# Attention and two expert layers on one core: the loop over experts put outside the loop over token groups

## The chip, the core and the metric

The kernel runs on one core of one Trainium2 chip. The metric is the time of one execution on the device in microseconds (us); of several runs the median is taken. The engines are TensorE (PE in the rows; PEld is its weight load), VectorE (DVE), ScalarE (ACT), GpSimd (POOL) and SyncE (SP), which here only issues transfers.

## The reference

Three stages follow one another: attention with a memory, a dense layer of two matrix products, and four experts of the same form whose results are mixed.

```python
# 1: q, k, v (2, 8, 576, 64); local is causal softmax attention
attn = g * mem_out + (1 - g) * local            # -> x (1152, 512)
# 2: dense layer, w_in (512, 2048), w_out (2048, 512)
r = np.maximum(x @ w_in, 0.0)
x = (r * r) @ w_out
# 3: E = 4 experts, w1 (4, 512, 1024), w2 (4, 1024, 512)
p = domain_probs / (domain_probs.sum(-1, keepdims=True) + 1e-09)
for e in range(E):
    h = np.maximum(x @ w1[e], 0.0)
    out += p[:, e:e + 1] * (h @ w2[e])
```

## The kernel before, in words

The 1152 tokens are nine tiles of 128. Attention and the dense layer run in three chunks of tiles; the experts run in two token groups, c = 0 with tiles 0 to 3 (512 tokens) and c = 1 with tiles 4 to 8 (640 tokens). The change is in the experts and in the last chunk of the dense layer, `ffn1(2, ...)`, which runs beside the first preparations for the experts.

**Blocks and pairs.** An expert's 1024 hidden units are cut into four blocks p of 256. `w2[e * 4 + p, half]` holds a block's weights as raw float32, 512 KB for the first matrix (half 0, "up") and 512 KB for the second (half 1, "down"). `pairs` lists (c, e, p): 32 pairs, the token group outermost, so that each block is met twice.

**A block's preparation.** `fetch(i, half)` (L873) issues the load of a raw block on SP. `square(i, half)` (L825) sums its squares on ACT, for an expert's scale. `w_power(e)` (L817) adds these sums up over partitions with a PE product by ones and makes powers of two of them on DVE (`power`); `prep_up` and `prep_down` scale by them. `prep_down` (L902) splits the down weights into a high and a low half in float16: two ACT copies (L832) and two DVE instructions (L833). `prep_up` (L879) does it for seven combinations of the up weights, since a product of 2 x 2 sub-blocks is done in seven sub-products: four sums on POOL into `ws` (L891 to L896, one buffer), two ACT copies into `wu` (L893, L899) and three DVE low parts (L888). The token side has the same splits: `tokens(c)` (L839) makes seven split operands `xs` out of four subtractions `tt` (L850), seven ACT copies and seven DVE instructions (L832, L833).

**A pair's products.** `up2(i)` (L912) issues seven products of six matmuls (L924) into PSUM banks taken in turn from `spots`; ACT copies two of them (p1 at L947, p5 at L953, which frees their banks), DVE adds the others up (L945), POOL adds one term (u4 at L954). `hidden(m)` (L936) then makes the hidden values: ACT's Relu gives the high half (L939), DVE the low half (L940). `down2(i)` (L1000) multiplies the hidden values by the down weights, three matmuls of 512 columns for each tile and half m (L1016), into one PSUM bank per tile (`o0` to `o4`); after an expert's last block `drain` (L1024) scales the bank and adds it to `acc` on DVE (L1029), and after the last expert issues the output transfer (L1035).

**Order.** PE executes in the order of the program. The other engines' instructions are put in order by a scheduler, which goes by priority in program order and by when it expects an instruction to be ready; an instruction under `tc.keep_in_program_order` keeps its place. Each engine executes its instructions strictly in the order that results, so that one that waits holds up all behind it. The loop at the end of the program makes one step for each pair i: the steps of `up2(i)` are spread among those of `down2(i - 1)`, and after each one a step of the next preparation is issued, with squares at fixed places:

```python
        fetch(i + 6, 0)
        fetch(i + 6, 1)
...
        ahead = chain(prep_down(i), prep_up(i + 1))
        for n, g in enumerate(steps):
            next(g)
            next(ahead, None)
            if n in (5, 7, 9, 11):
                square(*next(todo, (len(pairs), 0)))
```

Raw blocks have 6 and 7 buffers, `wu` has 2, the split down weights 2. In the last dense chunk the loop over `ffn1(2, ...)` issues the fetches of blocks 0 to 5 and the squares of blocks 0 to 3, the scale of expert 0, the splits of the first token group, the preparation of the first up weights, and in its last steps the products of the first pair (`up_0`). That chunk's own weights are rounded on ACT (L83) and their low half is made on POOL or DVE (L84); its Relu, square and split are L706, L707, L712 and L713, its matmuls L106 and L723.

## Time and profile before

| | us |
|---|---|
| median of 3 runs | 743.21 (741.28 to 744.14) |
| the profiled execution, its own time | 740.5 |
| its span, first to last instruction | 738.7 |
| PE busy | 686.9 (93%) |
| DVE busy | 549.1 (74%) |
| ACT busy | 430.2 (58%) |
| POOL busy | 241.4 (33%) |

The profile's times count from the first instruction of the span. A busy share is an average over stages: attention and the dense layer run until about 375 us, the first token group of the experts until about 525 us, the second to the end. In a row of the timeline the number in brackets is the idle time of the engine just before, with what ended it.

### The profile page before, as it was taken

How to read it: one execution, taken by the hardware profiler on the slowest of the kernel's cores; microseconds unless marked ns; L12 is line 12 of the kernel's file. 1: busy time of each engine (PE TensorE's matmuls, PEld its weight loads, DVE VectorE, ACT ScalarE, POOL GpSimd, SP SyncE). 2: the span in 40 equal slices, each digit the busy share in tenths (PEclk: the TensorE clock that was granted, in tenths of full speed). 3: DMA queues.
4: the chain of work that ended last, by engine and by line, in shares of the span. 5: the costliest groups of instructions: out<-in, count | busy, mean ns of one | idle time of the engine just before them, and what ended most of it. 6: DMA issues, size and time to landing. Idle time of an engine off the chain costs nothing.

```text
span 738.7 us, 12576 instructions
## 1 busy us (share of the span) xinstructions
PE 686.9 (93%) x4604; PEld 487.1 (66%) x4604; DVE 549.1 (74%) x1057; ACT 430.2 (58%) x844; POOL 241.4 (33%) x249
## 2 busy tenths in 40 slices
PE   6588899989899998999999989999999999999997
PEld 4466777767677787989865655566655555555553
DVE  4867858479989874746879968989787685867763
ACT  5687767376665534887776756655535353535341
POOL 1101101253533237645623433344432323141400
PEclk7799999999999999999999999999999999999999
DMA  9788765177885543685412323233342222100002
GB/s 286 229 297 289 254 219 180 58 262 222 196 197 122 122 114 83 238 302 169 131 59 93 108 85 115 87 113 94 109 168 75 100 81 91 58 1 1 1 1 71
DMA packets 65422, 101.25 MB, mean 137 GB/s; under 512 B 32656, under 2 KB 34704, under 8 KB 65360
## 3 DMA queue, kind: packets, MB, share of 16 engines
q1 hardware_dynamic: 65216, 100.45, 44.5%
q8 instruction: 36, 0.59, 0.3%
q14 instruction: 26, 0.21, 0.1%
q10 hardware_dynamic: 144, 0.00, 0.0%
HBM read 82.87 MB, written 10.75 MB: 127 GB/s over the span
## 4 chain that ended last, share of the span: by engine, by line
PE 52%; DVE 18%; ACT 11%; DMA 9%; issue 6%; POOL 3%; SPq 0%; DVEq 0%; ACTq 0%; POOLq 0%
PE o L1016 19%; PE pe L924 16%; DMA raw<-in_w 4%; PE y L723 3%; PE hpb L106 3%; PE pv L584 2%; DMA wraw<-w1s 2%; DVE bits L661 2%; PE y L721 2%; POOL w L84 2%; PE hpa L101 2%; DVE g L713 1%; ACT a L320 1%; DVE a L189 1%; PE sc L516 1%
## 5 line engine op out<-in xcount | busy, mean ns | idle before, releaser
L1016 PE MATMUL o<-w,g 128*128 128x512 f16 x864 | 218.5, 379 | 7.0 <-DVE g L940 3.8
L924 PE MATMUL pe<-xs,wu 128*128 128x256 f16 (+1 forms) x1344 | 196.5, 286 | 2.1 <-DVE h L945 2.0
L924 PEld LDWEIGHTS <-wu 128*128 128x128 f16 x1344 | 131.0, 98 | 70.3 <-issue 3.8
L1016 PEld LDWEIGHTS <-g 128*128 128x128 f16 x864 | 83.7, 98 | 77.8 <-DVE g L940 7.1
L84 POOL TENSOR_TENSOR w<-wraw,w 128x512 fp32r<-128x512 f32 x49 | 73.1, 1498 | 104.6 <-ACT w L83 104.3
L939 ACT ACTIVATE g<-h 128x512 f16<-128x512 f32 (+1 forms) x64 | 43.3, 677 | 105.7 <-DVE h L945 105.7
L723 PE MATMUL y<-g,w 128*128 128x512 f32 (+1 forms) x384 | 90.7, 372 | 1.5 <-ACT w L83 0.7
L954 POOL TENSOR_TENSOR u<-u,p 128x256 f32<-128x256 f32 (+1 forms) x32 | 32.3, 1011 | 132.7 <-ACT p L953 110.9
L723 PEld LDWEIGHTS y<-g,w 128*128 128x128 f32 x384 | 68.2, 189 | 9.7 <-ACT w L83 1.0
L940 DVE SCALAR_TENSOR_TENSOR g<-h,g 128x512 f16<-128x512 f32 (+1 forms) x64 | 50.4, 788 | 26.3 <-ACT g L939 26.0
L106 PE MATMUL hpb<-x,w 128*128 128x512 f32 x192 | 53.2, 414 | 4.7 <-DVE r L707 4.6
L945 DVE SCALAR_TENSOR_TENSOR h<-pe,u 128x256 f32<-128x256 f32 (+1 forms) x96 | 42.8, 451 | 19.8 <-PE pe L924 15.7
L891 POOL TENSOR_TENSOR ws<-raw 128x256 f32<-128x256 f32 x32 | 23.3, 727 | 101.9 <-issue 88.7
L888 DVE SCALAR_TENSOR_TENSOR wu<-ws,wpow,wu 128x512 f16<-128x512 f32 x64 | 50.9, 835 | 2.9 <-ACT wu L899 2.9
L833 DVE SCALAR_TENSOR_TENSOR w<-raw,wpow,w 128x512 f16<-128x512 f32 x64 | 48.0, 755 | 0.7 <-ACT w L832 0.6
L83 ACT ACTIVATE w<-wraw 128x512 fp32r<-128x512 f32 x64 | 39.5, 623 | 13.0 <-DMA wraw<-w1s 6.6
L106 PEld LDWEIGHTS hpb<-x,w 128*128 128x128 f32 x192 | 36.3, 196 | 13.6 <-DVE r L707 6.4
L832 ACT ACTIVATE w<-raw,wpow 128x512 f16<-128x512 f32 x64 | 44.6, 709 | 0.9 <-PE o L1016 0.9
L829 ACT ACTIVATE junk<-raw 128x1024 bf16<-128x1024 f32 x32 | 33.5, 1048 | 19.0 <-DMA raw<-in_w 18.9
L189 DVE CUSTOM_DVE_ANT_0 a<-sc,mask 128x384 f32<-128x384 f32 (+4 forms) x80 | 35.9, 477 | 11.1 <-PE sc L303 5.5
L204 POOL TENSOR_TENSOR xm<-xm,cf 128x512 f32<-128x512 f32 x9 | 10.6, 1184 | 102.1 <-ACT at L337 42.7
L106 PE MATMUL hpc<-x,w 128*128 128x384 f32 x192 | 37.3, 339 | 3.1 <-POOL w L84 2.0
(159 smaller groups left out, 1200.0 us busy)
## 6 DMA issues: line engine op xcount, KB each, us to landing
raw<-in_w SPq DMA_DIRECT2D x64, 512.0 KB, 3.4
w<-in_w SPq DMA_DIRECT2D x32, 512.0 KB, 4.4
wraw<-w1s SPq DMA_DIRECT2D x64, 256.0 KB, 3.1
w1s<-bits SPq DMA_DIRECT2D x32, 256.0 KB, 2.5
kraw<-in_kc SPq DMA_DIRECT2D x8, 576.0 KB, 4.1
vraw<-in_vc SPq DMA_DIRECT2D x8, 320.0 KB, 3.7
qraw<-in_qc SPq DMA_DIRECT2D x4, 512.0 KB, 4.9
out<-acc SPq DMA_DIRECT2D x8, 256.0 KB, 2.1
```

What stands on the lines that cost most here:

```text
L84: eng.tensor_sub(w[:, 1], raw, w[:, 0].bitcast(F32))
L106: nc.tensor.matmul(acc, lhsT=w[:, a, kk * P:(kk + 1) * P], rhs=xs_r[c][:, b, kk, :], start=(i == 0), stop=(i == 3 * NK - 1),)
L189: nc.vector.tensor_tensor_reduce(out=dst, in0=sc, in1=msk, op0=ALU.add, op1=ALU.max, scale=1.0, scalar=-3.0e38, accum_out=m)
L723: nc.tensor.matmul(yacc[d], lhsT=w[:, a, d * P:(d + 1) * P], rhs=g[:, b], start=(first and i == 0), stop=(last and i == 2),)
L832: nc.scalar.activation(out=w0, in_=x, func=AF.Copy, scale=s)
L833: nc.vector.scalar_tensor_tensor(out=w1, in0=x, scalar=s, in1=w0, op0=ALU.mult, op1=ALU.subtract)
L888: nc.vector.scalar_tensor_tensor(out=w[:, 1, ks], in0=x, scalar=s1, in1=w[:, 0, ks], op0=ALU.mult, op1=ALU.subtract)
L924: nc.tensor.matmul(acc, lhsT=w[:, wa, k, kk * P:kk * P + P], rhs=x[:, xb, kk], start=(m == 0), stop=(m == 5))
L939: nc.scalar.activation(out=g[:, 0], in_=hm, func=AF.Relu)
L940: nc.vector.scalar_tensor_tensor(out=g[:, 1], in0=hm, scalar=0.0, in1=g[:, 0], op0=ALU.max, op1=ALU.subtract)
L945: nc.vector.scalar_tensor_tensor(out=out, in0=acc, scalar=HID, in1=x, op0=ALU.mult, op1=ALU.add)
L1016: nc.tensor.matmul(outs[t], lhsT=g[:, gb, r:r + P], rhs=w[:, wa], start=(p == 0 and m == 1 and k == 0), stop=(p == 3 and m == 0 and k == 2),)
```

## The change

The loops over experts and token groups change places: `pairs` runs over e, then c, then p, so that a block is prepared once, into one of five `wu` buffers and one of five buffers for down weights, and used by both groups. `blocks` lists (e, p), and `fetch`, `square`, `prep_up` and `prep_down` go by block q. Raw blocks have four buffers each; a block's preparation itself issues the fetch of the block four later. The blocks of the next expert are squared in steps 1 to 4 of an expert's eight, pinned in program order, one at place 9 of a step and one at its end; its scale is made in step 5 and its blocks are prepared in steps 5, 6, 7 and 0. The splits of the second token group come in steps 2 and 3 of the whole loop. The fourth product bank (`o4`) is taken back for three steps of each first group. For an expert's last block `down2` goes tile by tile, and the sums of the second group get a place of their own (`late_acc`).

```diff
-    pairs = [(c, e, p) for c in range(2) for e in range(ne) for p in range(4)]
+    blocks = [(e, p) for e in range(ne) for p in range(4)]
+    pairs = [(c, e, p) for e in range(ne) for c in range(2) for p in range(4)]
...
-    def square(i, half):
-        if i < len(pairs):
-            c, e, p = pairs[i]
-            if c == 0:
-                nc.scalar.activation(out=junk2, in_=raws[i, half], func=AF.Square, accum_out=wsq[:, e, half, p:p + 1])
+    def square(q, half):
+        e, p = blocks[q]
+        tc.keep_in_program_order(
+            nc.scalar.activation(out=junk2, in_=raws[q, half], func=AF.Square, accum_out=wsq[:, e, half, p:p + 1])
+        )
...
-    def fetch(i, half):
-        if i < len(pairs):
-            _, e, p = pairs[i]
-            raw = raws[i, half] = xp.tile([P, 2 * DM], F32, tag=f"raw{half}", name=f"raw{half}", bufs=6 + half)
-            nc.sync.dma_start(out=raw, in_=w2[e * 4 + p, half])
+    def fetch(q, half):
+        if q < len(blocks):
+            raw = raws[q, half] = xp.tile([P, 2 * DM], F32, tag=f"raw{half}", name=f"raw{half}", bufs=4)
+            nc.sync.dma_start(out=raw, in_=w2[q, half])
...
-        w = wus[i] = xp.tile([P, 2, 7, 2 * P], F16, tag="wu", name="wu")
+        w = wus[q] = xp.tile([P, 2, 7, 2 * P], F16, tag="wu", name="wu", bufs=5)
...
+        fetch(q + 4, 0)
         low(w, s[:, 2:4], slice(5, 7))
...
-        w = wp.tile([P, 2, DM], F32R, tag="w0", name="w0").bitcast(F16)
+        if q % 5 == 4:
+            w = acp.tile([P, 2, DM], F32R, name="w2").bitcast(F16)
+        else:
+            w = wp.tile([P, 2, DM], F32R, tag=f"w{q % 5 % 2}", name="wd").bitcast(F16)
...
+        fetch(q + 4, 1)
+
+    def prep(q):
+        yield from prep_down(q)
+        yield from prep_up(q)
...
-            if 8 <= i < 56 and i % 4 == 0:
+            if 8 <= i < 40 and i % 4 == 0:
                 fetch((i - 8) // 8, i // 4 % 2)
...
+        if p == 3:
+            todo.sort(key=lambda x: 2 * x[0] - 3 * x[1])
...
+    late_acc = xyp.tile([P, NT - LAST, DM], F32, tag="x2", name="acc")
+    n_e = 2 * 4
...
-        fetch(i + 6, 0)
-        fetch(i + 6, 1)
-        todo = iter([(j, half) for j in {0: (), 1: (4, 5), 2: (6, 7)}.get(i, (i + 5,)) for half in range(2)])
...
-        ahead = chain(prep_down(i), prep_up(i + 1))
+        spots[3:] = [(ps_o, "o4")] if c == 0 and (p or not i) else []
...
+        step, ahead, todo = i % n_e, iter(()), []
+        if e == 0 and c == 0:
+            ahead = chain(prep_down(p), *([prep_up(p + 1)] if p < 3 else []))
+        elif i >= n_e - 3:
+            q = 4 * ((i - n_e + 3) // n_e + 1) + (i - n_e + 3) % n_e
+            if (i - n_e + 3) % n_e < 4 and q < len(blocks):
+                ahead = prep(q)
+        if 1 <= step <= 4 and e + 1 < ne:
+            todo = [(4 * (e + 1) + step - 1, half) for half in range(2)]
         for n, g in enumerate(steps):
             next(g)
-            next(ahead, None)
-            if n in (5, 7, 9, 11):
-                square(*next(todo, (len(pairs), 0)))
+            if step != 5 or n > 3:
+                next(ahead, None)
+            if n == 9 and todo:
+                square(*todo.pop(0))
...
-            if n == 14 and i < 4 * ne - 4 and i % 4 == 2:
-                w_power(pairs[i + 2][1], bank([P, 8], "wt").rearrange("p (m n) -> p m n", m=2))
-        if i >= 5 and steps:
-            next(side, None)
+            if (i == 2 and n % 3 == 2) or (i == 3 and n % 3 < 2):
+                next(side, None)
+            if n == 2 and step == 5 and e + 1 < ne:
+                w_power(e + 1, bank([P, 8], "wt").rearrange("p (m n) -> p m n", m=2))
         run(ahead)
+        if todo:
+            square(*todo.pop(0))
```

Three places of the order that results are shown, before and after; the line numbers are each program's own.

ACT before, in the loop's sixth step (L829 is a square, L939 the Relu of the hidden values, L947 and L953 the copies p1 and p5, L832 and L893 and L899 copies of weights):

```order
L829 ACTIVATE junk2_3277,wsq_3276<-raw0_4793 128x1024
L939 ACTIVATE g1_4766<-h1_4668 128x512
L829 ACTIVATE junk2_3277,wsq_3276<-raw1_4795 128x1024
L832 ACTIVATE w0_4812<-raw1_4137,wpow_3274 128x512
L939 ACTIVATE g0_4780<-h0_4667 128x512
L947 ACTIVATE p1_4799<-pe_4804 128x256
```

ACT after, in steps 4 and 5 of the second expert (L946 is the Relu, L954 p1, L960 p5, L833, L891 and L897 the copies of weights):

```order
L829 ACTIVATE junk2_3277,wsq_3276<-raw0_5078 128x1024
L946 ACTIVATE g1_5521<-h1_5444 128x640
L946 ACTIVATE g0_5536<-h0_5443 128x640
L829 ACTIVATE junk2_3277,wsq_3276<-raw1_5051 128x1024
L954 ACTIVATE p1_5546<-pe_5551 128x320
L833 ACTIVATE wd_5599<-raw1_4711,wpow_3274 128x512 x2
L891 ACTIVATE wu_5618<-raw0_4738,wpow_3274 128x768
L960 ACTIVATE p5_5547<-pe_5607 128x320
L897 ACTIVATE wu_5618<-ws_5619,wpow_3274 128x1024
L891 ACTIVATE wu_5716<-raw0_4835,wpow_3274 128x768
```

One square now stands ahead of the two Relus and one behind them; three copies that need the new expert's scale stand ahead of p5, and the copies of two blocks stand in one step.

POOL before, at the end of the dense layer (L891 to L896 are sums of up weights, block 1's and block 2's; L84 is the low half of the last dense block but one; L954 is u4 of the first pair):

```order
L896 TENSOR_TENSOR ws_4145<-raw0_3405,ws_4145 128x256
L84 TENSOR_TENSOR w1_3973<-wraw_3927,w1_3973 128x512
L891 TENSOR_TENSOR ws_4197<-raw0_3457 128x256
L895 TENSOR_TENSOR ws_4197<-raw0_3457 128x256
L892 TENSOR_TENSOR ws_4197<-ws_4197,raw0_3457 128x256
L896 TENSOR_TENSOR ws_4197<-raw0_3457,ws_4197 128x256
L954 TENSOR_TENSOR u4_4016<-u2_4014,p5_4013 128x256
```

POOL after, the same place (L889 to L894 are the sums, L961 is u4):

```order
L894 TENSOR_TENSOR ws_4138<-raw0_3405,ws_4138 128x256
L889 TENSOR_TENSOR ws_4190<-raw0_3457 128x256
L893 TENSOR_TENSOR ws_4190<-raw0_3457 128x256
L890 TENSOR_TENSOR ws_4190<-ws_4190,raw0_3457 128x256
L894 TENSOR_TENSOR ws_4190<-raw0_3457,ws_4190 128x256
L84 TENSOR_TENSOR w1_3965<-wraw_3919,w1_3965 128x512
L889 TENSOR_TENSOR ws_4318<-raw0_3506 128x256
L893 TENSOR_TENSOR ws_4318<-raw0_3506 128x256
L890 TENSOR_TENSOR ws_4318<-ws_4318,raw0_3506 128x256
L894 TENSOR_TENSOR ws_4318<-raw0_3506,ws_4318 128x256
L961 TENSOR_TENSOR u4_4010<-u2_4008,p5_4007 128x256
```

Block 2's four sums moved ahead of the dense layer's low half, and block 3's four ahead of the first pair's u4.

ACT after, the end of the dense layer up to p1 of the first pair (L83 is the dense layer's rounding, L706 and L712 its Relu and split; `ws_4138` and `ws_4190` are blocks 1 and 2, `raw0_3506` is block 3):

```order
L897 ACTIVATE wu_4137<-ws_4138,wpow_3274 128x1024
L891 ACTIVATE wu_4317<-raw0_3506,wpow_3274 128x768
L706 ACTIVATE r_3944<-hpc_3926 128x384
L833 ACTIVATE wd_4130<-raw1_3385,wpow_3274 128x512 x2
L712 ACTIVATE g_3947<-r_3944 128x384
L83 ACTIVATE w1_3965<-wraw_3919 128x512
L897 ACTIVATE wu_4189<-ws_4190,wpow_3274 128x1024
L706 ACTIVATE r_3983<-hpc_3968 128x384
L833 ACTIVATE wd_4299<-raw1_3482,wpow_3274 128x512 x2
L712 ACTIVATE g_3986<-r_3983 128x384
L83 ACTIVATE w1_4019<-wraw_3924 128x512
L954 ACTIVATE p1_4006<-pe_4011 128x256
```

Before, the copies of blocks 2 and 3 stood behind the first pair's first Relu; here both blocks have one ahead of p1 (`wu_4317`, `wu_4189`).

## Rows read from the trace of the kernel before

**Rows 1.** Busy time by stretch: stretch, length, then PE, PEld, DVE, ACT, POOL, clock, DMA.

```profile
377.00:525.00 148.00, 140.61 (x938) 91.01 (x937) 126.46 (x248) 91.97 (x159) 58.77 (x70) 1.00 0.30 97
525.00:724.00 199.00, 198.71 (x1182) 115.34 (x1180) 142.85 (x236) 85.22 (x130) 57.79 (x77) 1.00 0.18 59
```

**Rows 2.** Timeline of PE, dense layer: start, length, engine, line, shapes [idle before].

```profile
326.40 0.61 PE L106 MATMUL hpc<-x,w 128*128 128x384 f32 x2 [0.41 <-ACT w L83]
...
333.59 2.02 PE L106 MATMUL hpc<-x,w 128*128 128x384 f32 x10 [0.84 <-POOL w L84]
```

**Rows 3.** Timeline of ACT, dense layer and sixth step of the experts.

```profile
321.55 1.04 ACT L829 ACTIVATE junk<-raw 128x1024 bf16<-128x1024 f32 x1
...
325.73 1.14 ACT L83 ACTIVATE w<-wraw 128x512 fp32r<-128x512 f32 x2
...
428.12 1.06 ACT L829 ACTIVATE junk<-raw 128x1024 bf16<-128x1024 f32 x1 [5.33 <-DMA raw<-in_w]
```

**Rows 4.** Timeline of PE, experts' loop.

```profile
396.92 0.81 PE L924 MATMUL pe<-xs,wu 128*128 128x256 f16 x6 [0.26 <-DVE h L945]
...
409.26 0.61 PE L1016 MATMUL o<-w,g 128*128 128x512 f16 x2 [0.33 <-DVE g L940]
...
429.84 0.39 PE L1016 MATMUL o<-w,g 128*128 128x512 f16 x1 [0.96 <-ACT g L939]
...
533.33 1.79 PE L924 MATMUL pe<-xs,wu 128*128 128x320 f16 x12 [0.29 <-DVE h L945]
```

**Rows 5.** Groups by shape, 377 to 733 us: busy us, mean ns | idle before.

```profile
L888 DVE SCALAR_TENSOR_TENSOR wu<-ws,wpow,wu 128x512 f16<-128x512 f32 x60 | 47.0, 824 | 0.3 <-ACT wu L899 0.3
L833 DVE SCALAR_TENSOR_TENSOR w<-raw,wpow,w 128x512 f16<-128x512 f32 x60 | 44.5, 744 | 0.7 <-ACT w L832 0.6
L832 ACT ACTIVATE w<-raw,wpow 128x512 f16<-128x512 f32 x60 | 41.9, 709 | 0.9 <-PE o L1016 0.9
L899 ACT ACTIVATE wu<-ws,wpow 128x1024 f16<-128x1024 f32 x30 | 34.1, 1137 | 0.0
L888 DVE SCALAR_TENSOR_TENSOR wu<-raw,wpow,wu 128x768 f16<-128x768 f32 x29 | 29.7, 1023 | 6.1 <-ACT wu L893 5.6
L893 ACT ACTIVATE wu<-raw,wpow 128x768 f16<-128x768 f32 x29 | 27.0, 930 | 14.3 <-PE pe L924 11.1 <-DVE wpow L134 3.3
...
L940 DVE SCALAR_TENSOR_TENSOR g<-h,g 128x512 f16<-128x512 f32 x31 | 23.0, 741 | 14.2 <-ACT g L939 14.1
...
L945 DVE SCALAR_TENSOR_TENSOR h<-pe,u 128x256 f32<-128x256 f32 x45 | 18.2, 414 | 4.4 <-PE pe L924 3.1 <-POOL u L954 1.2
...
L829 ACT ACTIVATE junk<-raw 128x1024 bf16<-128x1024 f32 x16 | 16.8, 1051 | 18.4 <-DMA raw<-in_w 18.4
...
L833 DVE SCALAR_TENSOR_TENSOR xs<-tt,ypow,xs 128x640 f16<-128x640 f32 x4 | 4.4, 1088 | 0.0
...
L850 DVE TENSOR_TENSOR tt<-y 128x640 f32<-128x640 f32 x2 | 1.6, 818 | 0.0
```

**Rows 6.** Timeline of all engines, dense layer to experts.

```profile
360.56 1.15 ACT L899 ACTIVATE wu<-ws,wpow 128x1024 f16<-128x1024 f32 x1 [2.73 <-POOL ws L896]
...
364.30 0.95 PE L723 MATMUL y<-g,w 128*128 128x384 f32 x2 [0.74 <-ACT w L83]
...
364.32 1.56 POOL L84 TENSOR_TENSOR w<-wraw,w 128x512 fp32r<-128x512 f32 x1 [3.79 <-ACT w L83]
364.67 1.76 DVE L888 SCALAR_TENSOR_TENSOR wu<-ws,wpow,wu 128x512 f16<-128x512 f32 x1
...
366.51 0.73 POOL L891 TENSOR_TENSOR ws<-raw 128x256 f32<-128x256 f32 x1 [0.63 <-DVE wu L888]
...
371.46 0.81 PE L924 MATMUL pe<-xs,wu 128*128 128x256 f16 x6 [1.30 <-DVE h L945]
```

**Rows 7.** Timeline of all engines, end.

```profile
731.18 3.39 DVE L1029 SCALAR_TENSOR_TENSOR acc<-o,prs,acc 128x512 f32<-128x512 f32 x5 [2.41 <-PE o L1016]
731.96 3.62 SPq L1035 DMA_DIRECT2D out<-acc  x6
```

More of the change, by code (lines that the diff above doesn't have):

```diff
@@ L986, in attention_then_experts @@
                 next(up_0, None)
+        run(side)
         run(up_0)
@@ L1011, in down2 @@
         todo = [(t, m) for m in (1, 0) for t in range(t0, t1)]
+        if p == 3:
+            todo.sort(key=lambda x: 2 * x[0] - 3 * x[1])
         for t, m in todo:
-            g, w = gs[i, m], wds[i, m]
+            g, w = gs[i, m], wds[4 * e + p, m]
             r = (t - t0) * P
@@ L1025, in drain @@
         if e == 0:
-            acc[t] = acp.tile([P, DM], F32, tag=f"acc{i}", name="acc")
+            acc[t] = late_acc[:, i] if t >= EXPERT_CHUNKS[1][0] else acp.tile([P, DM], F32, tag=f"acc{i}", name="acc")
             nc.vector.tensor_scalar_mul(acc[t], outs[t], scale)
@@ L1036, in drain @@
                 r += n
+    late_acc = xyp.tile([P, NT - LAST, DM], F32, tag="x2", name="acc")
+    n_e = 2 * 4
     side = iter(())
-    spots.append((ps_o, "o4"))
-    for i in range(len(pairs)):
-        if pairs[i][0] and len(spots) > 3:
-            spots.pop()
-        fetch(i + 6, 0)
-        fetch(i + 6, 1)
-        todo = iter([(j, half) for j in {0: (), 1: (4, 5), 2: (6, 7)}.get(i, (i + 5,)) for half in range(2)])
-        if i:
-            late = [down2(i - 1)] * (2 * (EXPERT_CHUNKS[pairs[i - 1][0]][1] - EXPERT_CHUNKS[pairs[i - 1][0]][0]))
-            steps = spread([up2(i)] * 7, late, 0.25)
-        else:
-            steps = []
-        ahead = chain(prep_down(i), prep_up(i + 1))
+    for i, (c, e, p) in enumerate(pairs):
+        spots[3:] = [(ps_o, "o4")] if c == 0 and (p or not i) else []
+        late = []
+        if i:
+            t0, t1 = EXPERT_CHUNKS[pairs[i - 1][0]]
+            late = [down2(i - 1)] * (2 * (t1 - t0))
+        steps = spread([up2(i)] * (7 if i else 0), late, 0.25)
+        step, ahead, todo = i % n_e, iter(()), []
[7 more added lines that the diff above has]
+            todo = [(4 * (e + 1) + step - 1, half) for half in range(2)]
         for n, g in enumerate(steps):
             next(g)
-            next(ahead, None)
-            if n in (5, 7, 9, 11):
-                square(*next(todo, (len(pairs), 0)))
+            if step != 5 or n > 3:
+                next(ahead, None)
+            if n == 9 and todo:
+                square(*todo.pop(0))
             if n == 10 and i == 1:
@@ L1061, in attention_then_experts @@
                 side = tokens(1)
-            if n == 14 and i < 4 * ne - 4 and i % 4 == 2:
-                w_power(pairs[i + 2][1], bank([P, 8], "wt").rearrange("p (m n) -> p m n", m=2))
-        if i >= 5 and steps:
-            next(side, None)
+            if (i == 2 and n % 3 == 2) or (i == 3 and n % 3 < 2):
+                next(side, None)
+            if n == 2 and step == 5 and e + 1 < ne:
+                w_power(e + 1, bank([P, 8], "wt").rearrange("p (m n) -> p m n", m=2))
         run(ahead)
+        if todo:
+            square(*todo.pop(0))
+        if i == 3:
+            run(side)
     run(down2(len(pairs) - 1))
```

20 lines of the change are left out of this document (9 added, 11 removed).

## The prediction

> **What bounds the kernel now.** I read the busy time by stretch first [rows 1]. From 525 us to 724 us TensorE (PE) is busy 198.71 of 199 us at full granted clock: the second token group leaves nothing to win. From 377 to 525 us (the first group) it is busy 140.61 of 148 us, so 7.4 us are lost. I then listed every idle time of PE after 300 us. In the last dense layer there are three between 326.4 and 333.6 us, 2.43 us together [rows 2]; at the hand-over to the experts three more, among them 0.74 and 1.30 us [rows 6]; in the first three steps of the experts' loop three, 1.60 us together (0.26, 1.01, 0.33; first and last in [rows 4]); and from 429.84 to 533.33 us eleven, 6.00 us together (first and last in [rows 4]). More than these some 13 us no edit of this kind can win, for the matmuls stay the same in number and shape.
>
> Why PE waits there is told by ScalarE (ACT) [rows 3]. At 428.12 us it had stood idle 5.33 us until a raw weight block landed: a Square was next in its queue. Behind it stood the Relu that makes the hidden values, and PE waited 0.96 us for that Relu at 429.84 us. All sixteen squares of the loop cost ACT 18.4 us of such waiting [rows 5]. Near 325 us three squares (first 321.55 us) run ahead of the weight rounding at 325.73 us for which PE waits at 326.40 us [rows 2, 3].
>
> **The change, part by part.** I add up against the profiled execution (740.5 us; span 738.7 us) and move the difference to the median of the runs, 743.21 us, which lies 0.4% higher.
>
> *Prepared once.* Sixteen preparations of a weight block fall away. Each is on VectorE (DVE) 2 x 0.744 + 1.023 + 2 x 0.824 = 4.16 us, on ACT 2 x 0.709 + 0.930 + 1.137 = 3.49 us [rows 5], with four GpSimd (POOL) sums and two 512 KB loads. In sum 67 us of DVE, yet PE had waited for none of the second group's but 0.29 us [rows 1, 4]: worth nothing by itself. It pays in the first group. A step there takes (429.84 - 409.26 - 0.96) / 2 = 9.8 us [rows 4]; its own DVE work is 6 x 0.414 + 2 x 0.741 = 3.97 us [rows 5]. With a preparation that was 8.1 us before drains, without one there is air.
>
> *Squares, and loads earlier.* In the new order a raw block is asked for when its buffer's last block has been prepared, about a step or more before its square; nearly all squares stand behind a Relu or have had their data for a full step. I take all eleven idles as gone, **-6.0 us**. The end on the other side is -4.4: 1.6 us of them, late in the stretch, came from DVE's queue, where the second group's splits and drains met a preparation; those splits now come earlier. In the dense layer four squares and four loads leave and the others are spread one by one: of 2.43 us I take **-2.0** (ends -1 and -2.4).
>
> *The hand-over.* Here the change costs. With five buffers for prepared up-weights the scheduler pulls the preparations of all four blocks of the first expert ahead of the loop, before PE's last dense products. Before, ACT's second scaled copy of block 1 began at 360.56 us, after POOL's sums; the rounded weights of the last dense block but one reached PE at 364.30 us, and their low half was done by POOL at 364.32 + 1.56 = 365.88 us [rows 6]. Now one more 0.93 us copy stands on ACT ahead of that rounding, and on POOL four sums of block 2 stand ahead of that low half. They may start when DVE has read block 1's sums (360.56 + 1.14 for the copy + 2 x 0.74 = 363.2 us) and take 4 x 0.73 = 2.9 us, or 3.9 if one of them is held up once as DVE was at 364.67 us (1.76 instead of 0.74). The low half, 1.56 us, then ends at 367.7 to 368.7 us: **+1.8 to 2.8** there. Behind it the first expert copy on ACT (p1) queues after block 2's sums as well, so that a bank of PSUM comes free late and the loop's first products start about 2.9 us late. I take **+2.9**. The ends: 0, if the slack of two blocks that the dense layer has takes it up; +5.5, if all that is added on DVE ahead of the first hidden values (1.02 + 4 x 0.74 + 2 x 0.74) ends on PE.
>
> *Steps 1 to 3.* They lose most of their preparations (about 3 x 4.16 us) and gain all seven splits (near 1.09 us) and four subtractions (0.82 us) of the second token group, 10.5 us [rows 5]. DVE then has 3 x 3.97 + 10.5 + 1.5 for what is left of the last preparation = 23.9 us, and small scale work besides, in 29.5 us: nearly as full as with preparations (24.4 us). I leave the present 1.60 us of stalls: **0** (ends -1.6 and +2).
>
> *The three changes of expert.* The sum of squares is now taken in step 5 of each expert, and behind it ACT's queue holds two 0.709 us copies and one of 0.930 us that need its result, ahead of the copy p5 that frees a bank; two blocks are prepared in one step. The nearest rows are the idles of 0.26 and 0.33 us around the first change of expert [rows 4]: three times 0.33 is **+1.0**. Ends: 0, for steps of the second group have 12 us, and +7 (three times 2.35 us of copies). The rota of three and four banks now switches seven times instead of once, and at two of them a product comes into the bank of the one before with three matmuls between: **+0.2** (0 to 1).
>
> *The last products.* Tile by tile, four drains come sooner; the last tile is still the last. Five drains ended at 731.18 + 3.39 = 734.57 us and six output transfers were issued until 735.58 us [rows 7]: the last transfer can be issued a little sooner, **-0.3** (0 to -0.6).
>
> Sum: -6.0 - 2.0 + 2.9 + 0 + 1.0 + 0.2 - 0.3 = **-4.2 us**, which makes 739.0 us of 743.2.
>
> **A rule against the change.** At 364.67 us a DVE low part of 512 columns took 1.76 us where the form's mean is 0.824, while POOL's subtraction ran from 364.32 to 365.88 us [rows 5, 6]. The Trainium skill, page SBUF — State Buffer, section Who interferes with whom, says that a DVE instruction with two SBUF inputs and a GpSimd instruction that reads SBUF exclude each other for a whole instruction. The trace agrees here: the low part ended 0.55 us after POOL's. Pulling POOL's sums and DVE's low parts of several blocks into one stretch makes it bite oftener; by that rule the sum is rival C's instead of mine.
>
> **The rivals.**
> A, the forecast: 739.0 us; by the ends of its nearer terms 736.5 to 742.
> B, the crowd costs nothing: the dense layer's slack and the 12 us steps absorb it. For it speaks that the second group ran with a preparation in each step at 198.71 of 199 us [rows 1]. Then -6.0 - 2.0 - 0.3 = -8.3: 734.9 us.
> C, slower: POOL's sums and DVE's low parts exclude each other wherever two blocks are prepared together. Eight more sums by the first products x 0.73 = 5.8 us on DVE, 2.0 us that the full steps 1 to 3 can't absorb, and one sum, 0.73 us, at each of three changes: 5.8 + 2.0 + 2.2 = +10.0 over the forecast, 749.0 us. It decides from 4.2 us more than I allow. Against it: low parts take 0.824 us in the mean, the split halves of the same size 0.744 [rows 5], so few can have met a sum.
> D, the gain is only exchanged: squares were the last to be waited for but DVE's queue would have been late without them, so that only half of the 6.0 us goes, and the changes of expert cost 2 us: -3.0 - 2.0 + 2.9 + 2.0 = -0.1: 743.1 us. For it speaks that the idles behind a Relu are often followed by a second one behind DVE's half of the hidden values. It is also the case in which the change doesn't do what it says.
>
> **Chances.** A 0.42, B 0.25, D 0.19, C 0.14. A change of 0.5% (3.7 us) is about what a measurement of this kernel can tell from none. A lies just beyond it and is faster in 0.24 of its 0.42; B is faster, D nearly always the same, C slower but for a quarter of it. Faster 0.51, same 0.36, slower 0.13. The range from 733.5 to 746.0 us takes in A with its ends, D, most of B and the mild part of C; A alone would be 736.5 to 742.
>
> **What would show it.** Right: no ACT idle before squares in the loop; PE idle from step 5 on under 1.5 us in sum; PE idle of some 5 us in the 15 us around the first expert products, released by POOL's or DVE's work there, with POOL's low half of the last dense block but one some 2 us later against PE's own progress; DVE's busy sum about 65 us lower. Wrong: idles behind the hidden values at steps 5 and 6 of each expert (changes dearer than I say), or low parts of 1.5 us and more in rows (C), or no new idle at the hand-over (B).

## The result, and the profile after

The changed kernel takes 750.02 us (median of 5 runs, 747.41 to 752.03), the kernel before beside it 741.85 us (740.79 to 744.14). The ratio is 1.0102 with a 95% interval of 1.0067 to 1.0137: the change makes the kernel 1% slower. 739.0 us were forecast, faster, and 750.02 lies outside the range. The profiled execution took 751.65 us, its span 749.6, against 740.5 and 738.7 before.

The work became less, as meant: DVE is busy 499.1 us (549.1 before), ACT 381.7 (430.2), POOL 203.8 (241.4). The loss shows in the busy time by stretch of the changed kernel (columns as in [rows 1]):

```profile
288.00:295.00 7.00, 7.00 (x45) 5.78 (x43) 0.65 (x1) 1.61 (x4) 3.51 (x3) 0.53 0.03 13
...
369.00:377.00 8.00, 5.37 (x21) 3.70 (x22) 7.60 (x10) 4.06 (x7) 6.10 (x6) 0.57 0.45 133
...
533.00:537.00 4.00, 3.40 (x11) 1.59 (x12) 4.00 (x7) 3.04 (x6) 1.88 (x2) 0.57 0.22 88
```

Two things go together in the last two: PE idles (at 369 to 377 us it is busy 5.37 of 8 us), and the granted clock, the figure behind POOL's, stands at 0.57 in the mean, so for most of the stretch at 1.2 instead of 2.4 GHz. Before, it was at 1.00 from 377 to 724 us [rows 1]. The first stretch lies ahead of everything that was changed; the last section comes back to it.

Who is waited for is in the groups by shape of the changed kernel, 384 to 746 us (as in [rows 5]):

```profile
L1026 PE MATMUL o<-wd,g 128*128 128x512 f16 x702 | 177.8, 381 | 5.4 <-ACT g L946 3.7 <-DVE g L947 1.0 <-ACT y L728 0.6
...
L1026 PE MATMUL o<-w,g 128*128 128x512 f16 x162 | 41.0, 379 | 2.4 <-ACT g L946 1.9 <-DVE g L947 0.5
...
L829 ACT ACTIVATE junk<-raw 128x1024 bf16<-128x1024 f32 x24 | 25.1, 1044 | 0.0
```

The squares (L829) wait 0.0 us, where they had waited 18.4 [rows 5]. Yet the second products still wait for the Relu (L946), 5.6 us in sum. These are three pairs of idles, at 441, 533 and 627 us, one at each change of expert. The timeline of all engines at the first of them, changed kernel:

```profile
435.15 0.73 DVE L886 SCALAR_TENSOR_TENSOR wu<-ws,wpow,wu 128x512 f16<-128x512 f32 x1
...
436.02 1.38 POOL L889 TENSOR_TENSOR ws<-raw 128x256 f32<-128x256 f32 x1 [2.14 <-issue]
...
438.85 0.73 POOL L894 TENSOR_TENSOR ws<-raw,ws 128x256 f32<-128x256 f32 x1
...
439.61 1.15 ACT L897 ACTIVATE wu<-ws,wpow 128x1024 f16<-128x1024 f32 x1 [5.32 <-POOL ws L894]
440.66 0.72 ACT L946 ACTIVATE g<-h 128x640 f16<-128x640 f32 x1
...
441.44 0.39 PE L1026 MATMUL o<-wd,g 128*128 128x512 f16 x1 [1.86 <-ACT g L946]
...
442.33 0.61 PE L1026 MATMUL o<-wd,g 128*128 128x512 f16 x2 [0.51 <-DVE g L947]
```

Five `wu` buffers let the scheduler prepare block 5, the second of the next expert, a step ahead of its place. Its second copy on ACT (L897, 439.61 us) needs POOL's four sums; these could begin only when DVE had read block 4's sums out of the one `ws` buffer (435.15 + 0.73 = 435.88 us). ACT waits 5.32 us for them, and the Relu stands behind. It is the picture of [rows 3], where a square waited 5.33 us for its load ahead of the Relu: one wait has taken the place of the other.

The hand-over, timeline of PE, changed kernel:

```profile
365.38 0.83 PE L931 MATMUL pe<-xs,wu 128*128 128x256 f16 x6
368.15 0.44 PE L723 MATMUL y<-g,w 128*128 128x384 f32 x1 [1.94 <-ACT w L83]
369.80 0.69 PE L723 MATMUL y<-g,w 128*128 128x384 f32 x1 [1.21 <-DVE g L713]
372.31 0.69 PE L723 MATMUL y<-g,w 128*128 128x384 f32 x1 [1.83 <-POOL w L84]
372.81 1.50 PE L931 MATMUL pe<-xs,wu 128*128 128x256 f16 x6
...
383.26 0.81 PE L931 MATMUL pe<-xs,wu 128*128 128x256 f16 x6 [0.82 <-DVE h L952]
```

And POOL there, same kernel:

```profile
366.34 0.73 POOL L889 TENSOR_TENSOR ws<-raw 128x256 f32<-128x256 f32 x1 [2.78 <-DVE wu L886]
...
369.40 0.92 POOL L894 TENSOR_TENSOR ws<-raw,ws 128x256 f32<-128x256 f32 x1
370.29 1.97 POOL L84 TENSOR_TENSOR w<-wraw,w 128x512 fp32r<-128x512 f32 x1
```

Block 2's four sums now stand ahead of the low half of a dense weight (L84), which in [rows 6] came first; PE gets it at 372.3 us. By the end of the first two idles, of 1.94 and 1.21 us, the clock has fallen: one product takes 0.69 us at 369.80 us where it took 0.44 at 368.15, and six matmuls take 1.50 us at 372.81 us instead of 0.83. Two more idles, of 0.35 and 0.60 us, follow at the start of the loop (384.43 and 385.85 us). In the dense layer itself there are two idles of 0.40 and 0.60 us where [rows 2] have theirs, and a new one of 1.74 us just ahead of the hand-over, timeline of PE, changed kernel:

```profile
332.68 0.59 PE L106 MATMUL hpc<-x,w 128*128 128x384 f32 x2 [0.40 <-DVE r L707]
333.87 2.01 PE L106 MATMUL hpc<-x,w 128*128 128x384 f32 x10 [0.60 <-POOL w L84]
...
361.45 2.00 PE L106 MATMUL hpc<-x,w 128*128 128x384 f32 x10 [1.74 <-POOL w L84]
```

The end, all engines, changed kernel: the transfers are issued over 4.89 us instead of 3.62 [rows 7], since four of the five drains come earlier, and from PE's last product (738.49 + 6.87 us) to the end of the span it is 4.3 us instead of 5.0.

```profile
738.49 6.87 PE L1026 MATMUL o<-wd,g 128*128 128x512 f16 x30
...
741.64 4.89 SPq L1045 DMA_DIRECT2D out<-acc  x6
```

For the comparisons below I cut each profiled span into three stages: D, from the first product of the last dense chunk (295.67 us before, 297.76 after) to the first expert product; H, the hand-over, from there to the first product of pair 1; L, the loop, from there to the end of the span. (Rivals have letters too, and are called rivals where D, H or L could be mistaken.) What lies ahead of D differs by up to 4.3 us from one profile to another; no edit here reaches PE's instructions there. Each row's stages are of one execution, which lies up to 4 us off the median (e3's above it, e1's 3 us below).

| kernel | median us | ratio to before (95%) | D | H | L |
|---|---|---|---|---|---|
| before | 741.85 | 1 | 67.05 | 12.83 | 363.15 |
| changed | 750.02 | 1.0102 (1.0067 to 1.0137) | 67.62 | 17.88 | 366.34 |
| e1 before, squares held | 741.75 | 1.0016 (0.9993 to 1.0040) | 68.74 | 16.37 | 357.41 |
| e2 four `wu` buffers | 742.08 | 1.0018 (0.9997 to 1.0038) | 66.79 | 17.84 | 357.37 |
| e3 second copy held | 754.30 | 1.0183 (1.0153 to 1.0213) | 67.33 | 17.20 | 373.85 |
| e4 all copies held | 737.65 | 0.9971 (0.9955 to 0.9987) | 65.96 | 13.34 | 360.09 |
| e5 held, hand-over mended | 731.85 | 0.9879 (0.9855 to 0.9903) | 65.97 | 8.89 | 358.84 |
| e6 e5, no tile order | 731.81 | 0.9879 (0.9855 to 0.9903) | 66.48 | 8.88 | 359.58 |
| e7 four buffers, squares free | 737.62 | 0.9953 (0.9930 to 0.9976) | 65.16 | 18.66 | 355.83 |
| e8 four buffers, two `ws` | 738.60 | 0.9966 (0.9949 to 0.9983) | 68.43 | 15.97 | 356.20 |
| e9 before, held and mended | 734.88 | 0.9925 (0.9906 to 0.9945) | 67.87 | 8.88 | 358.71 |
| e10 e5 without POOL's sums | 728.96 | 0.9841 (0.9812 to 0.9870) | 64.53 | 8.88 | 356.40 |
| e11 first expert held, mended | 741.25 | 1.0018 (0.9996 to 1.0040) | 65.40 | 8.88 | 367.64 |

The medians of before ran from 739.7 to 741.85 us beside these kernels, so ratios are compared. Of the 10.9 us between the spans of before and after, 2.1 lie ahead of D, 0.6 in D, 5.0 in H and 3.2 in L.

### The profile page after: what moved, and what is told of

Read it like the earlier page. It is cut to its first block, busy times and chain, and to the rows that moved or that the text cites. A ratio compares the mean times of both kernels' runs of the same rounds, so it can differ in the third digit from the quotient of the medians.

```text
span 749.6 us, 12250 instructions
## 1 busy us (share of the span) xinstructions
PE 693.6 (93%) x4604; PEld 491.3 (66%) x4604; DVE 499.1 (67%) x977; ACT 381.7 (51%) x780; POOL 203.8 (27%) x185
## 5 line engine op out<-in xcount | busy, mean ns | idle before, releaser
L1026 PE MATMUL o<-wd,g 128*128 128x512 f16 x702 | 177.8, 381 | 5.4 <-ACT g L946 3.7
L946 ACT ACTIVATE g<-h 128x512 f16<-128x512 f32 (+1 forms) x64 | 43.6, 681 | 119.9 <-DVE h L952 119.8
L84 POOL TENSOR_TENSOR w<-wraw,w 128x512 fp32r<-128x512 f32 x49 | 73.7, 1510 | 103.0 <-ACT w L83 102.7
L723 PE MATMUL y<-g,w 128*128 128x512 f32 (+1 forms) x384 | 94.3, 383 | 5.0 <-ACT w L83 1.9
L961 POOL TENSOR_TENSOR u<-u,p 128x256 f32<-128x256 f32 (+1 forms) x32 | 29.3, 916 | 248.7 <-ACT p L960 240.9
L723 PEld LDWEIGHTS y<-g,w 128*128 128x128 f32 x384 | 70.6, 196 | 13.8 <-POOL w L84 2.2
L947 DVE SCALAR_TENSOR_TENSOR g<-h,g 128x512 f16<-128x512 f32 (+1 forms) x64 | 49.2, 770 | 29.8 <-ACT g L946 29.1
L83 ACT ACTIVATE w<-wraw 128x512 fp32r<-128x512 f32 x64 | 39.7, 623 | 14.0 <-PE y L723 7.4
L960 ACT ACTIVATE p<-pe 128x256 f32<-128x256 f32 (+1 forms) x32 | 12.9, 404 | 61.4 <-PE pe L931 61.4
L952 DVE SCALAR_TENSOR_TENSOR u<-pe,u 128x256 f32<-128x256 f32 (+1 forms) x32 | 14.5, 453 | 44.3 <-PE pe L931 44.3
L1026 PE MATMUL o<-w,g 128*128 128x512 f16 x162 | 41.0, 379 | 2.4 <-ACT g L946 1.9
L713 DVE TENSOR_TENSOR g<-r,g 128x512 fp32r<-128x512 f32 (+1 forms) x32 | 35.5, 1109 | 10.1 <-ACT g L712 10.0
L886 DVE SCALAR_TENSOR_TENSOR wu<-ws,wpow,wu 128x512 f16<-128x512 f32 x32 | 27.1, 868 | 20.8 <-ACT wu L897 20.8
L101 PE MATMUL hpa<-y,bits 128*128 128x256 f32 x128 | 37.1, 408 | 1.6 <-DVE g L707 0.9
```

The lines of the kernel that those rows point to most:

```text
L83: nc.scalar.activation(out=w[:, 0], in_=raw, func=AF.Copy)
L84: eng.tensor_sub(w[:, 1], raw, w[:, 0].bitcast(F32))
L101: nc.tensor.matmul(acc, lhsT=w[:, kk * P:(kk + 1) * P], rhs=first_x[:, kk, :], start=(kk == 0), stop=(kk == NK - 1),)
L713: nc.vector.tensor_sub(g[:, 1], r, g[:, 0].bitcast(F32))
L723: nc.tensor.matmul(yacc[d], lhsT=w[:, a, d * P:(d + 1) * P], rhs=g[:, b], start=(first and i == 0), stop=(last and i == 2),)
L946: nc.scalar.activation(out=g[:, 0], in_=hm, func=AF.Relu)
```

## The experiments

Theory A: the loss comes from the order of instructions alone, from preparations drawn ahead of what PE waits for. Rival C: VectorE and GpSimd stretch each other wherever two blocks are prepared together.

**e1. One part alone: the squares held, in the kernel before.**

```diff
-                nc.scalar.activation(out=junk2, in_=raws[i, half], func=AF.Square, accum_out=wsq[:, e, half, p:p + 1])
+                tc.keep_in_program_order(
+                    nc.scalar.activation(out=junk2, in_=raws[i, half], func=AF.Square, accum_out=wsq[:, e, half, p:p + 1])
+                )
```

> The kernel before, with its squares alone held to their written place on ScalarE (its loops, buffers and transfers untouched). Theory A (the change lost by order: preparations drawn ahead on ScalarE, GpSimd and VectorE at the hand-over and at the three changes of expert; the squares themselves were the gain): the row of squares keeps its 16 but loses most of its 18.4 us of waiting, the six us of TensorE idles at 429.84 to 533.33 go, 735 to 738 us. Rival C (VectorE and GpSimd shut each other out and stretch each other's instructions, wherever they stand): also faster, since nothing of the crowd is in this kernel. Rival D (the squares' wait is only exchanged for another wait): 741 to 743 us, no difference.

Measured: 741.75 us, a ratio of 1.0016, no difference, as rival D had it; but not for its reason. In L the kernel gains 5.7 us, as A expected. The eleven idles are gone but for 0.83 and 0.29 us, and so are the 1.60 us of the first steps, against one new wait of 2.64 us for a held square; the 1.9 us of the gain that this doesn't make up stand in no idle time. Stage H loses 3.5 us and stage D 1.7, with a fall of the clock in each (0.50 from 333.2 to 336.4 us in D). Timelines of POOL and PE in this kernel:

```profile
363.49 0.73 POOL L893 TENSOR_TENSOR ws<-raw 128x256 f32<-128x256 f32 x1 [2.78 <-ACT w L834]
...
366.57 0.92 POOL L898 TENSOR_TENSOR ws<-raw,ws 128x256 f32<-128x256 f32 x1
367.45 1.71 POOL L84 TENSOR_TENSOR w<-wraw,w 128x512 fp32r<-128x512 f32 x1
...
369.22 0.69 PE L723 MATMUL y<-g,w 128*128 128x384 f32 x1 [1.82 <-POOL w L84]
```

It is the changed kernel's picture: with no loop moved, two `wu` buffers and nothing edited on POOL, block 2's sums stand ahead of the low half. Four squares ran on ACT between 356 and 370 us before and none does here (the loop now has 24 squares instead of 16), which suggests, but doesn't show, that the scheduler expected the sums sooner.

**e2. Block 5 can't be drawn ahead.**

```diff
-        w = wus[q] = xp.tile([P, 2, 7, 2 * P], F16, tag="wu", name="wu", bufs=5)
+        w = wus[q] = xp.tile([P, 2, 7, 2 * P], F16, tag="wu", name="wu", bufs=4)
```

> The changed kernel with four buffers for the up weights in place of five, so that block 5 of the next expert cannot be prepared a step ahead. Theory A: the pairs of TensorE idles of 1.86 and 0.51 us at 441, 533 and 627 us go, and with them the half-speed stretch behind the one at 533; the hand-over is unchanged (its idles still about 6.7 us): 7 to 9 us below the changed kernel, 741 to 743 us. Rival C: VectorE's low parts stay as long as they are and the stall moves to the next product, at most 2 us below the changed kernel, 748 to 750 us.

Measured: 742.08 us, as A expected (by the ratios 6.2 us under the changed kernel, where A had 7 to 9), and L is 9.0 us shorter. ACT at the change of expert in this kernel:

```profile
433.62 0.74 ACT L946 ACTIVATE g<-h 128x640 f16<-128x640 f32 x1 [2.86 <-DVE h L952]
434.62 0.94 ACT L891 ACTIVATE wu<-raw,wpow 128x768 f16<-128x768 f32 x1 [0.27 <-PE pe L931]
435.84 0.74 ACT L946 ACTIVATE g<-h 128x640 f16<-128x640 f32 x1 [0.28 <-DVE h L952]
...
438.03 1.14 ACT L897 ACTIVATE wu<-ws,wpow 128x1024 f16<-128x1024 f32 x1
```

The same two copies (L891, L897) are there, but the second behind both Relus. PE waits at none of the three changes. H is as in the changed kernel (17.84 against 17.88 us), as A had it.

**e3. Half a remedy.**

```diff
-        nc.scalar.activation(out=w[:, 0, 3:7], in_=s, func=AF.Copy, scale=s1)
+        tc.keep_in_program_order(nc.scalar.activation(out=w[:, 0, 3:7], in_=s, func=AF.Copy, scale=s1))
```

> The changed kernel with ScalarE's second copy of each up weight block held to its written place, the first copy still free. Where block 5 is drawn ahead at a change of expert its second copy still stands ahead of the two Relus, so this leaves that wait as it is. Theory A: idles of 1.8 us and more stay at the three changes of expert; only the hand-over changes, since the last dense layer's weight copy now comes before block 1's second copy, by 0 to 4 us: 746 to 750 us. Rival C: no change at either place, 749 to 751 us. A further rival, E (any pin costs ScalarE time): slower than 752 us.

Measured: 754.30 us. The three idles stay (1.87 us each), as A had it, but the kernel is slower than A allowed. Rival E named the time but not the cause, for e4 holds more and is faster. At the hand-over ACT and PE now show:

```profile
371.74 1.15 ACT L897 ACTIVATE wu<-ws,wpow 128x1024 f16<-128x1024 f32 x1 [3.14 <-POOL ws L894]
372.79 0.36 ACT L954 ACTIVATE p<-pe 128x256 f32<-128x256 f32 x1
...
373.20 1.44 PE L931 MATMUL pe<-xs,wu 128*128 128x256 f16 x6 [3.96 <-ACT p L954]
```

The dense weight comes earlier, but p1, which frees a bank, still stands behind a copy that waits for POOL's sums; further on PE waits 3.59 us for a copy of the dense layer's result (L728), behind the next one. The clock falls at each of these two waits and behind two of the three changes of expert, where in the changed kernel it fell behind one.

**e4. All of ACT's preparation held:** the two copies of the up weights (L891, L897), and in `prep_down` the copies of the down weights.

```diff
-        nc.scalar.activation(out=w[:, 0, 0:3], in_=u[:, 1:4], func=AF.Copy, scale=s1)
+        tc.keep_in_program_order(nc.scalar.activation(out=w[:, 0, 0:3], in_=u[:, 1:4], func=AF.Copy, scale=s1))
...
-        nc.scalar.activation(out=w0, in_=x, func=AF.Copy, scale=s)
+        (tc.keep_in_program_order if pin else (lambda x: x))(nc.scalar.activation(out=w0, in_=x, func=AF.Copy, scale=s))
```

> The changed kernel with all of ScalarE's weight preparation held to its written place (both copies of the up weights and the copies of the down weights). Theory A: at the hand-over p1 and the Relus come before the preparation of blocks 1 to 3, and at a change of expert before block 5's copies, so both losses go: the hand-over's idles fall from 6.75 to 3 us or less, the half-speed stretch behind them goes (2 to 3 us), the 7.1 us of idles at the three changes and some 1.5 us of half speed behind the second go, less what the pins themselves cost: 735 to 740 us, below the kernel before. Rival C: low parts of VectorE stay stretched and the wait moves from ScalarE to VectorE, 746 to 750 us.

Measured: 737.65 us, 0.3% under the kernel before. The waits at the changes are gone with five buffers too, so the order was at fault and not the buffers' number. At the hand-over PE now waits at one place, timeline of PE in this kernel:

```profile
375.51 0.39 PE L931 MATMUL pe<-xs,wu 128*128 128x256 f16 x2 [4.30 <-DVE wd L834]
376.56 2.32 PE L931 MATMUL pe<-xs,wu 128*128 128x256 f16 x10 [0.66 <-DVE wu L886]
```

Held in place, block 0's down weights and block 1's up weights come too late. That was more than the 3 us A expected there, and the clock fell behind it (0.50 from 376.0 to 379.4 us).

**e5. The hand-over mended, on top of e4.**

```diff
-        side, up_0 = chain(tokens(0), prep_up(0)), None
+        side, up_0, ahead_0 = chain(tokens(0), prep_up(0)), None, chain(prep_down(0), prep_up(1))
...
                 next(up_0, None)
+                next(ahead_0, None)
...
-            ahead = chain(prep_down(p), *([prep_up(p + 1)] if p < 3 else []))
+            ahead = chain(prep_down(p), *([prep_up(p + 1)] if p < 3 else [])) if p else ahead_0
```

> The changed kernel with all of ScalarE's weight preparation held as in the run before, and block 0's down weights and block 1's up weights written between the first expert products of the last dense steps instead of behind them. Theory A (the loss and the remedy are order alone): the 4.30 and 0.66 us that TensorE waited at 375.51 and 376.56 for those two blocks fall to 1.5 us or less, since ScalarE stood idle for 3.2 us and GpSimd for 10 us just ahead of them; the rest stays as with all held (737.65 us): 733.5 to 736 us. Rival H: the copies now stand ahead of the hidden values of pair 0 and cost there what they save behind: 736.5 to 739 us.

Measured: 731.85 us, 1.2% under the kernel before and a little under A's range. H is 8.89 us and PE waits for nothing in it. This is the best version that computes all.

**e6. e5 without the tile order.**

```diff
-        if p == 3:
-            todo.sort(key=lambda x: 2 * x[0] - 3 * x[1])
```

> The same kernel without the tile by tile order of the last products, all else equal. The forecast's own term for that order was 0.3 us gained, the two traces show 0.7 us between TensorE's last product and the end of the span: this kernel 0.3 to 1.0 us slower than the one with it; under rival I (the stores overlap anyway) no difference.

Measured: 731.81 us, no difference that can be seen: either ratio is known to 0.24%, 1.8 us, so 0.3 to 1.0 us could hide in it, and this doesn't decide between the two. In the profiles PE's last product lies 5.0 us ahead of the end of the span, with the order 4.3: the rows show the 0.7 us, the medians can't.

**e7. The squares not held, with e2's four buffers.**

```diff
-        tc.keep_in_program_order(
-            nc.scalar.activation(out=junk2, in_=raws[q, half], func=AF.Square, accum_out=wsq[:, e, half, p:p + 1])
-        )
+        nc.scalar.activation(out=junk2, in_=raws[q, half], func=AF.Square, accum_out=wsq[:, e, half, p:p + 1])
```

> The changed kernel with four buffers for the up weights and the squares not held to any place. It tells what the hold is worth inside the new loops. If the earlier loads alone end the squares' waiting (theory J: each block is now loaded some eight steps ahead), the row of squares stays at or under 1 us of idle and the time is that of four buffers with the hold, 741 to 743 us. If it is the hold (theory K), the squares are drawn ahead to where their loads have not landed, wait 5 us and more in sum, and TensorE's idles ahead of the hidden values come back: 744 to 749 us.

Measured: 737.62 us, a ratio of 0.9953. Neither J nor K. The squares wait again, 12.1 us in L as K said, but L is no longer than with the hold (355.83 against 357.37 us), and PE waits for no Relu in L. So the hold is worth nothing in L of the kernel with four buffers. Why the whole is 0.65% under e2 isn't settled: 2.2 us of the 4.5 between the two spans lie ahead of D.

**e8. Two `ws` buffers**, with e2's four `wu`. Two with five `wu` were not run.

```diff
-        s = xp.tile([P, 4, 2 * P], F32, tag="ws", name="ws", bufs=1)
+        s = xp.tile([P, 4, 2 * P], F32, tag="ws", name="ws", bufs=2)
```

> The changed kernel with four buffers for the up weights and two in place of one for GpSimd's sums. Theory A (order): at the hand-over the sums of blocks 1 to 3 go still further ahead and stand in front of the dense layer's last low part on GpSimd as before, idles of 5 us and more, 740 to 744 us. Rival G (the single buffer is the cause): ScalarE's second copies no longer wait 4.9, 2.3 and 3.9 us, TensorE's idles at the hand-over fall under 3 us, 736 to 739 us.

Measured: 738.60 us, a ratio of 0.9966, 0.5% under e2. Rival G is right in part: H falls by 1.9 us, and PE's three waits in the dense products there from 4.77 to 2.80 us; but D grows by 1.6, and the order stays crowded. One buffer is a part of the cause at the hand-over, not all of it.

**e9. The kernel before with e1's hold and the remedies of e4 and e5**, nothing of its loops moved. In its loop the last edit reads:

```diff
-        ahead = chain(prep_down(i), prep_up(i + 1))
+        ahead = chain(prep_down(i), prep_up(i + 1)) if i else ahead_0
```

> The kernel before, its loops, buffers and transfers untouched (every weight block still loaded and prepared twice), with its squares and all of ScalarE's weight preparation held to their written places, and block 0's down weights and block 1's up weights written between the first expert products of the last dense steps. It tells what the loop order itself is worth once the order of instructions is mended. Theory A (order is all; TensorE bounds the loop either way, so the 50 us of VectorE and 48 us of ScalarE that the loop change saves lie beside it): within 3 us of the changed kernel with the same edits (731.85 us), 730 to 736 us. Rival L (preparing once is what makes room): VectorE, busy 85% in the stretch from 400 to 525 us, holds TensorE up; 737 to 743 us.

Measured: 734.88 us, in A's range, though by the ratios a little more than 3 us over e5. L is as long as in e5 (358.71 and 358.84 us), though every block is loaded and prepared twice. Of the 0.46% between the two ratios, some 3.4 us, 1.9 us stand in D, where this profile's clock fell (0.50 from 335.1 to 338.4 us) and e5's didn't. The loops' new order, which takes 50 us off DVE, shortens L by nothing.

**e10. The price of POOL's company:** e5 without the four sums.

```diff
-        s = xp.tile([P, 4, 2 * P], F32, tag="ws", name="ws", bufs=1)
-        nc.gpsimd.tensor_add(s[:, 0], u[:, 0], u[:, 3])
-        nc.gpsimd.tensor_sub(s[:, 1], s[:, 0], u[:, 1])
+        s = u
...
-        nc.gpsimd.tensor_sub(s[:, 2], u[:, 1], u[:, 0])
-        nc.gpsimd.tensor_sub(s[:, 3], u[:, 2], s[:, 1])
```

> The held kernel with the mended hand-over, with GpSimd's four sums of each up weight block left out (the raw block is copied and subtracted in their place), so that part of the computation is missing. It prices GpSimd's company in VectorE's and ScalarE's work. Theory A: the waits for the sums are gone already, the low parts of VectorE fall from 0.83 to some 0.75 us each, beside TensorE: 0 to 1.5 us under 731.85 us. Rival C (the two engines shut each other out, and that sets the time): 3 us and more under it, 729 us or less.

Measured: 728.96 us, 0.4% under e5; the intervals overlap a little. The 2.9 us are more than A had said (1.5 at most) and stand at the edge of C's range (729 us or less). Groups by shape, 430 to 733 us, of e5 and then of this kernel:

```profile
L886 DVE SCALAR_TENSOR_TENSOR wu<-ws,wpow,wu 128x512 f16<-128x512 f32 x22 | 17.7, 826 | 0.0
```

```profile
L886 DVE SCALAR_TENSOR_TENSOR wu<-raw,wpow,wu 128x512 f16<-128x512 f32 x22 | 15.9, 745 | 0.0
```

The two means, 826 and 745 ns, are not the price of a sum. Of e5's 22 low parts nineteen take 735 to 747 ns and three, one at each change of expert, 1.35 us; these three run beside POOL's u4 (L961). None meets a sum: with one `ws` buffer the sums begin when these parts have read it. The first of the three is the second of the two parts in this row, timeline of all engines in e5:

```profile
434.78 2.01 DVE L886 SCALAR_TENSOR_TENSOR wu<-ws,wpow,wu 128x512 f16<-128x512 f32 x2
435.26 0.98 POOL L961 TENSOR_TENSOR u<-u,p 128x320 f32<-128x320 f32 x1 [4.35 <-ACT p L960]
```

The Trainium skill (SBUF — State Buffer, Who interferes with whom) says that such a pair exclude each other for a whole instruction; the trace agrees, for each of the three ends 0.55 us after u4. PE waits for none of them. At another place of e5 a sum does cost PE something: DVE's half of the hidden values (L947) takes 1.21 us beside it, where the mean in [rows 5] was 0.74, and PE waits for it.

```profile
394.26 1.30 POOL L890 TENSOR_TENSOR ws<-ws,raw 128x256 f32<-128x256 f32 x1
...
394.90 1.21 DVE L947 SCALAR_TENSOR_TENSOR g<-h,g 128x512 f16<-128x512 f32 x1
...
396.17 0.61 PE L1027 MATMUL o<-wd,g 128*128 128x512 f16 x2 [1.01 <-DVE g L947]
```

Without the sums this idle is 0.21 us, and PE's idles in L are 2.4 us in sum instead of 4.3. So the sums cost the mended kernel some 3 us (by the profiles 2.4 in L and 1.4 in D), a part of it by C's mechanism; how large a part isn't shown. It is not what slowed the changed kernel at the changes of expert: the mended one keeps its sums there and loses nothing.

**e11. Only the hand-over mended:** e5, with the copies held for the first expert's blocks alone; in `prep_down` likewise.

```diff
-        tc.keep_in_program_order(nc.scalar.activation(out=w[:, 0, 0:3], in_=u[:, 1:4], func=AF.Copy, scale=s1))
+        held = tc.keep_in_program_order if q < 4 else (lambda x: x)
+        held(nc.scalar.activation(out=w[:, 0, 0:3], in_=u[:, 1:4], func=AF.Copy, scale=s1))
```

> The changed kernel with five buffers, with the mended hand-over and the preparation of the first expert's four blocks alone held to its written place; that of the other three experts is free as in the changed kernel. Theory A (two losses, each of its own place): the hand-over is as short as with all held, 8.9 us, and the idles of 1.86 and 0.51 us stay at the three changes of expert, with a stretch at half speed behind one or more of them: 7 to 9.5 us over the kernel with all held (731.85 us), 739 to 741.5 us. Rival M (one loss: the crowd of the hand-over sets what is drawn ahead later): the changes mend too, 732 to 735 us.

Measured: 741.25 us, 9.4 over e5. H is 8.88 us, and the wait at the change of expert is back, timelines of ACT and PE in this kernel:

```profile
429.57 1.15 ACT L898 ACTIVATE wu<-ws,wpow 128x1024 f16<-128x1024 f32 x1 [5.32 <-POOL ws L895]
...
431.40 0.39 PE L1028 MATMUL o<-wd,g 128*128 128x512 f16 x1 [1.87 <-ACT g L947]
```

The two losses stand each in its own place: mending the changes alone (e2, by four buffers) or the hand-over alone (e11) each leaves a ratio of 1.0018, mending both (e5, by the hold) 0.9879. One point of A's missed: the clock stayed at 1.00 behind all three idles.

## Why the prediction was wrong

It went wrong at seams that it had named, and not by its reading of what bounds the kernel: two losses there were taken too small and a gain in the dense layer didn't come. Between the sum, -4.2 us, and the spans, +10.9, lie 15.1 us: 7.6 at the changes of expert, 2.6 in the dense layer, 2.1 at the hand-over, and 2.1 ahead of D, which no edit touches; the rest is smaller terms.

- **"Squares, and loads earlier", -6.0: right, and spent.** The eleven idles are gone (squares' wait 0.0), and e1 gives 5.7 us for the hold alone. e7 shows that the hold was not what the new loop needed.
- **"The three changes of expert", "three times 0.33 is +1.0": the step that failed.** It measured 7.1 us of idles (3 x (1.86 + 0.51)), and about 1.5 more at half clock behind the second (an estimate from 3.40 us of busy time at 0.57; from that change to the next it is 1.3 us longer than in e11, whose clock stayed). I looked for the wait at p5, behind copies that need the new scale. It stood ahead of the Relu, at a copy that waits for POOL's sums, because five buffers let block 5 go ahead. I had used the five buffers for the hand-over only. The upper end, +7, had the size but another mechanism, so that it came near is luck. e2, e4 and e11 show it.
- **"The hand-over", +2.9: right in kind, too small.** Block 2's sums do stand ahead of the low half on POOL, which ends 6.9 us after the first expert product (before 3.2), 3.7 later where I had 1.8 to 2.8. H measured +5.0, inside the end of +5.5: 3.1 us more idle (5.80 against 2.73) and some 2 us at half clock, a cost that no term had. And e1 shows that it doesn't need the five buffers that I gave as its cause.
- **Dense layer, -2.0: wrong.** D's idles are 2.74 us, they were 2.43: squares went, but the largest (1.74 us) is now released by POOL's low half.
- **"Steps 1 to 3", 0:** all 1.60 us of stalls went, the end of -1.6; the new 0.35 and 0.60 us at the loop's start stand against them.
- **The rota of banks, +0.2:** one wait of 0.96 us, at 570 us.
- **The last products, -0.3:** 0.7 us in the rows, too little for the medians to tell (e6).
- **"Prepared once", "worth nothing by itself": right.** e9 shows it for L. DVE's busy time fell by 50.0 us, not by the 65 that I had given as a sign.

The time came out at rival C's 749.0 us, but in the main not by C's mechanism. e2 takes the loss in L away with every sum still there, and in e5 low parts of 1.35 us stand at the changes and PE waits for none. What C priced is there in small: at each change the first of block 5's four sums takes 1.38 us instead of 0.73, within ACT's wait of 5.32 us. That few low parts of [rows 5] had met a sum, as I argued against C, was right: the long ones there (1.21 to 1.35 us) ran beside u4. At the hand-over C's share stays open: block 2's sums take 3.98 us (366.34 to 370.32), the 3.9 of my upper case, and the low half behind them 1.97 us instead of 1.56; mending the order (e5) ends the whole loss there, but no run separates the two. Rival D's idea, a gain exchanged for another wait, is what happened, with a wait dearer than the one removed.

My signs had this case right: I had written that idles behind the hidden values at the changes of expert would show them dearer than I said.

## What to carry to other kernels

Where a scheduler orders by readiness, a deeper buffer or a freed engine also lets later work go ahead of urgent work; ask of every such copy what it will wait for and who stands behind it in the strict queue. Look at each seam (hand-over, change of weights) on each engine, since PE's small waits there add up to more than a changed loop saves; a few instructions held to their place, and urgent preparations written where ACT is idle, won 1.2%; without the loops' new order the same remedies won 0.75% (e9). Half a hold can be worse than none (e3), and where TensorE already bounds a stage, 50 us less on VectorE buy nothing.
